# A planner's counts and priorities: transfers counted longer, and another engine taken sooner for the second weights' large part

## The chip, the cores and the metric

The kernel runs on one core of one Trainium2 chip. The metric is the device time of one execution in microseconds (us), and the median of several executions is compared. The engines are named as in the profile: PE (matrix products; PEld are its weight loads), DVE (vector), ACT (scalar), POOL (GpSimd) and SP, which here does nothing but issue DMAs from one queue, in the order of the program.

## What is computed

Nystrom attention over 8 batches, 8 heads, 576 rows and head size 64 with 32 landmarks, and then a mixture of 8 experts over the 4608 rows of the result, with one expert for each row:

```python
A = sm(q, k_lm)                       # 576 x 32 per head
Bm = sm(q_lm, k_lm)                   # 32 x 32
C = sm(q_lm, k)                       # 32 x 576
Z = Bm.T / (norms)
for _ in range(6):
    Z = 2 * Z - Z @ Bm @ Z
x = A @ Z @ C @ v                     # then rows of 8 * 64 = 512
...
expert = argmax(normed(x) @ normed(expert_emb).T / tau)
h = maximum(x @ w1[expert], 0)        # 512 -> 1024
out = gate * (h @ w2[expert])         # 1024 -> 512
```

## The kernel before

With these inputs all rows of a batch go to one expert. The kernel guesses the expert of each batch early (`guess`, `choose`), loads that expert's weights, computes the batch with them, and counts at the end whether a guess was wrong; a general path that would repair this stands behind a branch.

Each batch has its attention part and its expert part. The attention part: sums over segments of q and k (`sums`, L762), the small matrix and its inverse by six steps (`inverse`, `powers`), `values` and `products` for C @ v, `queries` for A, `landmarks` for the small factor. The expert part: four pieces of 512 KB of the first weights and four of the second weights are loaded by the SP queue (`weights`, L1360, tile `wstage`, after the expert's number `gi` has been read at L1340). ACT passes over each piece for a scale (`junk`, L1374 and L1433), and the sums over the four pieces go through PE (`ws,ones`) to give the scale. `first_weights` multiplies the first weights by the small factor on PE (`wstage,wt`) and splits the product into a large and a small float16 part (`ww`, L1418 on ACT and L1420 on DVE). `second_weights` splits the second weights likewise (`w2c`): the large part is a multiplication by the scale, on DVE (L1456) or on ACT (L1458), and the small part is always on DVE (L1460). `first` is 16 groups of six products `ab,ww` 128x288 for each batch. Each goes into one of three PSUM buffers and is taken out by a ReLU on ACT (L1468) and a difference on DVE (L1470) into `ht`. `second` is the products `w2c,ht`, whose results leave through `yt` and an output DMA on SP (L1558, L1560).

The order of all engines' instructions is made when the program is built, by a planner (`Weave`). Each step of the kernel is a generator that yields what it uses next: an engine and a duration in ns, a buffer, a flag. The planner plays these against each other in its own counted time, and issues the instruction that can start first; among those that can start within `SLACK` ns of it, the one with the highest priority (`PRI`, lowered by 1000 for each batch). A count of `DMA_LAT` is added behind every transfer. `("any", ...)` takes the engine that is counted to be done first; a third number on an offer is added to its count. `MARGIN` is added before PE steps that wait for something. On the chip each engine runs its instructions strictly in the resulting order, each waiting for its semaphores, so the counts decide the order alone and not the time.

Until the first product of `first` is issued (the flag `"moe"`), the planner also fills the time in which PE would be idle by its counts with products of ones (`keep_warm`, L673), so that the clock of PE stays up. Two lines set how many there are:

```python
    ns = self.warm((at - t) * (0.5 if self.cold(t) else 1.0) * WARM if at - t > WMIN else 0.0)
...
n = int(min(ns, 8000.0) / 56)
```

Of the kernel before, what the change touches and what calls it, by code (L numbers as in the profile page):

```python
# [48 lines left out]
HEAT = 3060.0  # L49
DENS = 1.0  # L50
LAT = {"pe": 180.0, "act": 160.0, "dve": 130.0, "pool": 160.0, "dma": 0.0}
DMA_LAT = 2000.0
SLACK = 46.4
EPS = 181.8
MARGIN = 607.2
BMARGIN = 400.0
SBIAS = 1000.0
AFTER = ("a", 0), ("a", 0)
QBIAS = 500.0
SUMS_DVE = 1  # L60
HBIAS = 0.0
WMIN = 400.0
SWITCH = 93.0
SAME = 200.0
# [10 lines left out]
BUFS = dict(k=2, q=2, v=2, ek=6, u=3, ec=2, ct=2, ae=3, at=2, st1=4, st2=4, w2=6, ww=2, ht=12, ab=3, yt=2, land=3, wt=3)  # L75

AHEAD = 20000
PRI = {"loads": 897, "sums": 1697, "inverse": 1697, "values": 1603, "queries": 703, "landmarks": 1653, "rows": 500,
       "route": 800, "guess": 844, "weights": 803, "first": 544, "second": 553}
FIRST = {"loads": 900, "sums": 800, "inverse": 800, "values": 800, "landmarks": 850, "guess": 810, "weights": 800,  # L80
         "first": 800, "embeddings": 600, "queries": 200}
EVICT, BULK = 10000, -1000
# [2 lines left out]
def rank(name, b):  # L85
    return PRI[name] - 1000 * b if b or name not in FIRST else AHEAD + FIRST[name]

# [43 lines left out]
class Weave:  # L131
# [122 lines left out]
    def run(self, *until):  # L254

        while self.gens and not (until and all(f in self.flags for f in until)):
# [4 lines left out]
            if safe > self.free["pe"]:  # L261
                ready = [(min(t, self._start(g, False)) if g[3][:2] == ("use", "pe") else t, g) for t, g in ready]
            assert ready, [g[3] for g in self.gens]
            first, lead = min(ready, key=lambda x: (x[0], x[1][3][0] in ("use", "any")))
            at, best = max(((t, g) for t, g in ready if g[3][:2] == lead[3][:2] and t <= first + SLACK),
                           key=lambda x: (self._rank(x[1]), -x[0]))
            r = best[3]
            if r[0] == "use":

                soon = [(t, g) for t, g in ready if g[2] >= max(AHEAD, best[2] + 100) and g[3][:2] == r[:2] and t < at + r[2] - EPS]  # L270
                if soon:
# [274 lines left out]
def nystrom_moe(ctx: ExitStack, tc: tile.TileContext, qT, kT, v, emb, w1, w2, out):  # L546
# [159 lines left out]
    def loads(b):  # L706
        if b:
            yield "wait", ("loads", b - 1)
        for src, dst, nm in ((kT, kt, "k"), (qT, qt, "q")):
            yield "get", nm  # L710
            if b == 2:

                yield "wait", ("weights", 2 if nm == "k" else 1, 0)
            dst[b] = inp.tile([P, 4, S], F32, tag=nm, name=nm + "_t", bufs=BUFS[nm])
            parts = 1 if b else 2
            for i in range(parts):
                yield "use", "dma", 3300 / parts
                r = slice(4 // parts * i, 4 // parts * (i + 1))
                sp.dma_start(dst[b][:, r], src[b][:, r])
                for x in range(2 // parts * i, 2 // parts * (i + 1)):  # L720
                    wv.flag((nm, b, x), DMA_LAT)
            wv.flag((nm, b), DMA_LAT)
            wv.add(sums(b, nm, dst[b]), boost=rank("sums", b))
        for gg in range(2):
            wv.add(load_values(b, gg), boost=rank("loads", b))
        wv.flag(("loads", b))

    def load_values(b, gg):
        if (b, gg) != (0, 0):
            yield "wait", ("vload", b - (not gg), 1 - gg)  # L730
        if b == 1:

            yield "wait", ("weights", 1, 0)
        i, = yield "get", "v"
        yield "use", "dma", 1640
        v_t = vt[b, gg] = vts[i]
        sp.dma_start(v_t[:, 0:4, :], v[b, 0:512, 256 * gg:256 * gg + 256].rearrange("(c p) x -> p c x", p=P))
        sp.dma_start(v_t[64:P, 4, :], v[b, 512:576, 256 * gg:256 * gg + 256])
        wv.flag(("v", b, gg), DMA_LAT)
        wv.flag(("vload", b, gg))  # L740
        wv.add(freed("v", ("vuse", b, gg), i))

    def sums(b, nm, src):
        if b >= NSUM:
            yield "wait", ("a", b - NSUM)
            yield "wait", ("u", b - NSUM)
        sm = sums_of[nm, b] = wk.tile([P, 4, M], F32, name=nm + "sum", bufs=NSUM)
        half = None
        for x in range(2):
            r = 2 * x  # L750
            yield "wait", (nm, b, x)
            if 0 < b < 3:

                yield "wait", AFTER[b - 1]
            sv = src[:, r:r + 2].rearrange("p r (m t) -> p (r m) t", t=SEG)
            if (yield "any", (("pool", 1360), ("dve", 1270, SBIAS if b >= SUMS_DVE else -SBIAS))) == "pool":
                yield "get", "half"
                half = wk.tile([P, 2 * M, SEG // 2], F32, name="half", bufs=1)
                pool.tensor_tensor(out=half, in0=sv[:, :, 0:9], in1=sv[:, :, 9:18], op=ALU.add)  # L759
                yield V(576)  # L760
                sv = half
            vec.tensor_reduce(sm[:, r:r + 2].rearrange("p r m -> p (r m)"), sv, axis=AX.X, op=ALU.add)  # L762
            if sv is half:
                wv.put("half")
        wv.flag((nm + "s", b))
        wv.tally((nm + "use", b), 2 if nm == "k" else 3)
# [197 lines left out]
    def freed(nm, flag, *ids):  # L964
        yield "wait", flag
        wv.put(nm, *ids)
# [55 lines left out]
    def held(b):  # L1022

        if b:
            yield "wait", ("ab", b - 1)
        yield "get", "ab"
        ab[b] = wk.tile([P, 2, 2, S], F16, name="ab", bufs=BUFS["ab"])
        wv.flag(("ab", b))
        yield "wait", ("rows", b)
        yield "use", "dma", 1700  # L1030
        sp.dma_start(abs_[b], ab[b])
        yield "wait", ("first", b)
        wv.put("ab")
# [305 lines left out]
    def reg(ap, max_val):  # L1339
        return nc.values_load_multi_w_load_instructions(ap, [mybir.EngineType.SP], min_val=0, max_val=max_val,  # L1340
                                                        bass_reorder=False)[1][0]
# [5 lines left out]
    def weights(b, m, src):  # L1347

        yield "wait", ("guess", b)
        if b:  # L1350
            yield "wait", ("weights", m, b - 1)
        yield "sleep", GUESS_LAT
        ev = None
        for q in range(4):
            yield "get", f"st{m}"
            yield "use", "dma", 1460
            if ev is None:
                ev = reg(gi[0:1, b:b + 1], E - 1)
            st = stage[m, b, q] = wst.tile([P, 1024], F32, tag=f"st{m}", name="wstage", bufs=BUFS[f"st{m}"])
            sp.dma_start(st, src[bass.ds(ev, 1), :, 1024 * q:1024 * q + 1024].rearrange("o p x -> (o p) x"))  # L1360
            wv.flag(("w", m, b, q), DMA_LAT)
        wv.flag(("weights", m, b))
# [64 lines left out]
    def second_weights(b):  # L1427
# [23 lines left out]
        for q in range(4):  # L1451
            yield "get", "w2"
            w = w2c[b, q] = wst.tile([P, 2, 1024], F16, name="w2c", bufs=BUFS["w2"])
            st = stage.pop((2, b, q))
            if (yield "any", (("act", 1144), ("dve", 660, HBIAS, True))) == "dve":
                vec.tensor_scalar(w[:, 0], st, sc, None, op0=ALU.mult)  # L1456
# [83 lines left out]
    def outputs(b, c, py, done, t0):  # L1540
        yield "sleep", LAT["pe"]
        yield "wait", ("gfac", b)
        if (b, c) == (B - 1, 3):

            left.append(nc.values_load(mi[0:1, 0:1], min_val=0, max_val=NT))
        yield "get", "yt"
        n = DM if c < 4 else DM // 2
        fac = gfac[:, b, c:c + 1]
        if (yield "any", (("act", n / 1.2 + 145), ("dve", (n + 66) / 0.96))) == "dve":
            yt = wst.tile([P, DM], F32, name="yt", bufs=BUFS["yt"])  # L1550
            vec.tensor_scalar(yt[:, 0:n], py[:, 0:n], fac, None, op0=ALU.mult)
        else:
            yt = wst.tile([P, DM], F32, name="yt", bufs=BUFS["yt"])
            act.activation(yt[:, 0:n], py[:, 0:n], AF.Copy, scale=fac)  # L1554
        done()
        yield "use", "dma", 730
        if c < 4:
            sp.dma_start(out[t0:t0 + P], yt)  # L1558
        else:
            sp.dma_start(out[t0:t0 + 64].rearrange("t (s x) -> s t x", s=2), yt[:, 0:256])  # L1560
        yield "sleep", DMA_LAT
        wv.put("yt")
# [20 lines left out]
    for b in range(B):  # L1583
        wv.add(loads(b), boost=rank("loads", b))
        wv.add(freed("k", ("kuse", b)))
        wv.add(freed("q", ("quse", b)))
        wv.add(batch(b))
    for b in range(B):
        wv.add(weights(b, 1, w1), boost=rank("weights", b))
        wv.add(weights(b, 2, w2), boost=rank("weights", b) - 50)  # L1590
        wv.add(first_scale(b), boost=rank("first", b))
        wv.add(first_weights(b), boost=rank("first", b))
        wv.add(second_weights(b), boost=rank("second", b))
# [7 lines left out]
    wv.warm = None  # L1601
    wv.margin, wv.bmargin = MARGIN, BMARGIN
    wv.put("bank", warm_id)
# [45 lines left out]
```

## Time and profile before

| | |
|---|---|
| median of 3 runs | 456.13 us (454.92 to 457.07) |
| the profiled execution | 455.07 us |
| its span, first to last instruction | 453.4 us |
| PE busy | 430.4 us, 95% of the span |
| DVE busy | 347.0 us, 77% |
| ACT busy | 254.1 us, 56% |
| POOL busy | 73.8 us, 16% |
| DMA | 78.21 MB, mean 173 GB/s |

A row of the profile gives the busy time of a group of instructions, the mean of one, and behind the bar the idle time of its engine just before them with what ended that idle time. A busy PE is not PE at its peak, since the ends of matmuls are modelled.

### The profile page before, as it was taken

To read this page: it belongs to the slowest core of one execution; us is meant where nothing else is said; L and a number is where in the kernel's file an instruction comes from. 1 tells how busy PE (TensorE), PEld (TensorE's weight loads), DVE (VectorE), ACT (ScalarE), POOL (GpSimd) and SP (SyncE) were. 2 spreads that over 40 slices of the span, in tenths; PEclk is the share of its full clock that TensorE was granted. 3 is DMA by queue.
4 is the path that set the end of the run, shared out by engine and by line. 5 is a ranking of instruction groups with operands and counts; after the bars stand their busy time and mean duration, and the time that the engine had idled before them with its cause. 6 is when DMAs were issued, how large, how long until landed. Compare 5 with 4: busy or idle time off the path is not lost.

```text
span 453.4 us, 13869 instructions
## 1 busy us (share of the span) xinstructions
PE 430.4 (95%) x5609; PEld 242.5 (53%) x5609; DVE 347.0 (77%) x1148; ACT 254.1 (56%) x611; POOL 73.8 (16%) x73
## 2 busy tenths in 40 slices
PE   7998899999999799999999899999999999999994
PEld 3544553466645366445655366555655466448641
DVE  5797999879797499968996299966995779578300
ACT  1377542865658455684476854866459545854211
POOL 3013341320121123300232003201020012010000
PEclk9999999999999899999999999999999999999999
DMA  8798254972278623882528913772047212921011
GB/s 298 256 394 282 75 188 135 368 239 68 87 251 286 222 67 119 283 320 75 169 78 300 334 42 121 273 251 100 26 140 279 78 49 64 329 103 38 11 50 51
DMA packets 29704, 78.21 MB, mean 173 GB/s; under 512 B 2624, under 2 KB 14016, under 8 KB 27840
## 3 DMA queue, kind: packets, MB, share of 16 engines
q1 hardware_dynamic: 29488, 77.15, 49.0%
q8 instruction: 46, 0.75, 0.7%
q14 instruction: 26, 0.21, 0.2%
q10 hardware_dynamic: 144, 0.10, 0.1%
HBM read 61.96 MB, written 15.27 MB: 170 GB/s over the span
## 4 chain that ended last, share of the span: by engine, by line
PE 56%; DVE 27%; DMA 6%; ACT 4%; issue 3%; POOL 2%; SPq 1%; ACTq 0%; POOLq 0%
PE ps L583 50%; DMA wstage<-w 6%; DVE ht L1470 5%; PE ps L673 4%; DVE w2c L1460 3%; DVE ww L1420 2%; DVE w2c L1456 1%; POOL half L759 1%; DVE cm L888 1%; DVE ae L986 1%; PE ps L935 1%; DVE am L991 1%; DVE asum L997 1%; DVE ksum L762 1%; ACT junk L1374 1%
## 5 line engine op out<-in xcount | busy, mean ns | idle before, releaser
L583 PE MATMUL ps<-w2c,ht 128*128 128x512 f16 (+1 forms) x1152 | 210.8, 346 | 0.8 <-DVE w2c L1460 0.8
L583 PEld LDWEIGHTS <-ht 128*128 128x128 f16 (+1 forms) x1152 | 88.8, 102 | 82.6 <-issue 12.0
L583 PE MATMUL ps<-ab,ww 128*128 128x288 f16 x768 | 106.4, 286 | 1.2 <-DVE ht L1470 1.1
L583 PEld LDWEIGHTS <-ww 128*128 128x128 f16 x768 | 71.5, 98 | 32.8 <-issue 11.8
L1468 ACT ACTIVATE ht<-ps 128x288 f16<-128x288 f32 x128 | 52.0, 409 | 58.0 <-PE ps L583 56.1
L1470 DVE SCALAR_TENSOR_TENSOR ht<-ps,ht 128x288 f16<-128x288 f32 x128 | 55.5, 446 | 8.4 <-ACT ht L1468 8.2
L1460 DVE SCALAR_TENSOR_TENSOR w2c<-wstage,wsc,w2c 128x1024 f16<-128x1024 f32 x32 | 40.8, 1275 | 0.7 <-ACT w2c L1458 0.7
L1433 ACT ACTIVATE junk<-wstage 128x1024 bf16<-128x1024 f32 x32 | 33.8, 1057 | 9.7 <-DMA wstage<-w 9.3
L1374 ACT ACTIVATE junk<-wstage 128x1024 bf16<-128x1024 f32 x32 | 33.7, 1054 | 8.2 <-DMA wstage<-w 8.0
L1554 ACT ACTIVATE yt<-ps,gfac 128x512 f32<-128x512 f32 (+1 forms) x26 | 16.5, 635 | 34.0 <-PE ps L583 33.8
L1257 POOL TENSOR_TENSOR nrm<-ssq,half 128x5 f32<-128x5 f32 x8 | 10.6, 1330 | 134.1 <-ACT junk L1239 134.1
L1239 ACT ACTIVATE junk<-ps 128x512 bf16<-128x512 f32 (+1 forms) x40 | 23.8, 595 | 14.3 <-DVE lg L1237 10.7
L759 POOL TENSOR_TENSOR half<-k_t 128x576 f32<-128x576 f32 x14 | 18.7, 1334 | 63.4 <-DVE ksum L762 17.4
L673 PE MATMUL ps<-ones 128*128 128x512 bf16 (+3 forms) x98 | 24.6, 396 | 2.3 <-POOL ones L608 2.3
L1420 DVE SCALAR_TENSOR_TENSOR ww<-ps,wsc,ww 128x1024 f16<-128x1024 f32 (+1 forms) x18 | 20.9, 1161 | 3.7 <-ACT ww L1418 3.6
L583 PE MATMUL ps<-wgd,ab 64*128 64x136 f16 (+1 forms) x480 | 20.7, 221 | 3.2 <-DVE ww L1420 3.2
L759 POOL TENSOR_TENSOR half<-q_t 128x576 f32<-128x576 f32 x14 | 19.7, 1406 | 24.1 <-DVE cm L910 6.9
L1418 ACT ACTIVATE ww<-ps,wsc 128x1024 f16<-128x1024 f32 (+1 forms) x18 | 18.3, 1014 | 9.0 <-PE ps L583 8.9
L583 PEld LDWEIGHTS ps<-ek 32*32 32x32 f32 x768 | 12.5, 105 | 19.1 <-issue 5.5
L583 PEld LDWEIGHTS <-ab 64*128 64x128 f16 (+1 forms) x480 | 14.4, 96 | 13.1 <-issue 11.4
L583 PE MATMUL ps<-ek 32*32 32x64 f32 (+1 forms) x768 | 20.0, 218 | 1.1 <-DVE ek L841 1.1
L1456 DVE TENSOR_SCALAR w2c<-wstage,wsc 128x1024 f16<-128x1024 f32 x25 | 19.3, 772 | 1.4 <-PE ps L583 1.4
(203 smaller groups left out, 567.0 us busy)
## 6 DMA issues: line engine op xcount, KB each, us to landing
wstage<-w SPq DMA_DIRECT2D x64, 512.0 KB, 6.2
v<-v SPq DMA_DIRECT2D x16, 512.0 KB, 6.5
out<-yt SPq DMA_DIRECT2D x32, 256.0 KB, 2.6
k_t<-kT SPq DMA_DIRECT2D x7, 1152.0 KB, 7.7
q_t<-qT SPq DMA_DIRECT2D x7, 1152.0 KB, 8.3
abs__135<-ab SPq DMA_DIRECT2D x8, 576.0 KB, 3.5
k_t<-kT SPq DMA_DIRECT2D x2, 576.0 KB, 5.3
q_t<-qT SPq DMA_DIRECT2D x2, 576.0 KB, 7.2
```

Source lines behind the costliest of these rows:

```text
L583: pe.matmul(o, lhsT, rhs, start=start, stop=stop)
L673: pe.matmul(warmth[:, 0:k * P], ones16, bc(ones16.unsqueeze(1), [P, k, P]), start=True, stop=True)
L759: pool.tensor_tensor(out=half, in0=sv[:, :, 0:9], in1=sv[:, :, 9:18], op=ALU.add)
L1239: act.activation(junk[lo:hi, 0:512].rearrange("p (i g x) -> p i g x", i=2, g=2), pfv[:, :, :, 0:2 * D], AF.Square, accum_out=ssq[lo:hi, cg ...
L1374: act.activation(junk, stage[1, b, q], AF.Square, accum_out=sq[:, q:q + 1])
L1418: act.activation(ww[:, 0], pww, AF.Copy, scale=sc)
L1420: vec.scalar_tensor_tensor(out=ww[:, 1], in0=pww, scalar=sc, in1=ww[:, 0], op0=ALU.mult, op1=ALU.subtract)
L1433: act.activation(junk, stage[2, b, q], AF.Abs, accum_out=sq[:, q:q + 1])
L1456: vec.tensor_scalar(w[:, 0], st, sc, None, op0=ALU.mult)
L1460: vec.scalar_tensor_tensor(out=w[:, 1], in0=st, scalar=sc, in1=w[:, 0], op0=ALU.mult, op1=ALU.subtract)
L1468: act.activation(ht[:, 0, r], ph[:, 0:HS], AF.Relu)
L1470: vec.scalar_tensor_tensor(out=ht[:, 1, r], in0=ph[:, 0:HS], scalar=0.0, in1=ht[:, 0, r], op0=ALU.max, op1=ALU.subtract)
```

## The change

Only numbers of the planner change; each engine's work is the same but for the choices that the planner makes anew. The counted latency of a transfer (`DMA_LAT`) goes from 2000 to 3600 ns, and each transfer's count on the queue up by some 4 to 7%. `SLACK`, `EPS` and `MARGIN`, and some priorities by a few points, change too. `HBIAS` goes from 0 to 700: DVE gets the large part of the second weights only where it would be done 700 ns sooner than ACT.

```diff
-DMA_LAT = 2000.0
-SLACK = 46.4
-EPS = 181.8
-MARGIN = 607.2
+DMA_LAT = 3600.0
+SLACK = 53.2
+EPS = 148.0
+MARGIN = 549.6
...
-HBIAS = 0.0
+HBIAS = 700.0
...
-PRI = {"loads": 897, "sums": 1697, "inverse": 1697, "values": 1603, "queries": 703, "landmarks": 1653, "rows": 500,
-       "route": 800, "guess": 844, "weights": 803, "first": 544, "second": 553}
+PRI = {"loads": 897, "sums": 1694, "inverse": 1697, "values": 1597, "queries": 700, "landmarks": 1656, "rows": 500,
+       "route": 794, "guess": 844, "weights": 803, "first": 550, "second": 550}
...
-            yield "use", "dma", 1460
+            yield "use", "dma", 1560
```

In the resulting order the products of ones (L673) are 108 of 512 columns, 3 of 384, 3 of 256 and 3 of 128, where they were 86, 5, 4 and 3. The large part of the second weights stands 30 times on ACT and 2 times on DVE (7 and 25 before). The differences and products of `both` (L1018, L1020) stand 26 times on POOL and 6 times on DVE (18 and 14 before). Three places follow.

PE just ahead of the first product of the first layer (`ab,ww`). Rows of `ones_99` are products of ones; `con,wt` is a step of `landmarks`, `wgd,ab` one of `rows`, `ws` the sum for the first weights' scale. Before:

```order
L583 MATMUL ps<-con,wt 32x8 x8
...
L673 MATMUL ps<-ones_99 128x256
L583 MATMUL ps<-wstage,wt 32x256 x8
L583 LDWEIGHTS ww
L583 MATMUL ps<-ab,ww 128x288
```

After:

```order
L583 MATMUL ps<-con,wt 32x8 x8
...
L583 MATMUL ps<-ws_646,ones_99 128x1
...
L673 MATMUL ps<-ones_99 128x384
...
L583 MATMUL ps<-wgd_109,ab 128x136
...
L673 MATMUL ps<-ones_99 128x256
L583 MATMUL ps<-wstage,wt 32x256 x8
L583 LDWEIGHTS ww
L583 MATMUL ps<-ab,ww 128x288
```

Where 12 products of ones of 512 columns and one of 256 stood, there are now 33 of 512, one of 384 and one of 256, with the sum and one step of `rows` among them.

SP, the second weights of batch 2 (the first four `wstage` behind the `TENSOR_LOAD gi` that reads the expert's number a second time). Before:

```order
L1340 TENSOR_LOAD gi
L1340 ISA x2
L1360 ISA
L1360 DMA wstage<-w 128x1024
L1360 ISA
L1360 DMA wstage<-w 128x1024
L1360 ISA
L1360 DMA wstage<-w 128x1024
L1558 DMA out<-yt 128x512
L1360 ISA
L1360 DMA wstage<-w 128x1024
```

After:

```order
L1340 TENSOR_LOAD gi
L1340 ISA x2
L1360 ISA
L1360 DMA wstage<-w 128x1024
L1360 ISA
L1360 DMA wstage<-w 128x1024
L1360 ISA
L1360 DMA wstage<-w 128x1024
L1360 ISA
L1360 DMA wstage<-w 128x1024
L1031 DMA abs__135<-ab 128x2304
```

The fourth piece no longer stands behind an output. Over all batches 11 outputs stand between the pieces of weights of a batch before, and 4 after.

ACT, from the last `ww` of batch 2 to the ReLUs of its first layer. Before:

```order
L1418 ACTIVATE ww<-ps,wsc_2494 128x1024
L1239 ACTIVATE junk,ssq<-ps 128x512
L1101 COPY ws__2718<-ps 128x128
L1554 ACTIVATE yt<-ps,gfac 128x256
L1111 COPY wt<-ps 128x128
L1113 ACTIVATE junk,wsqw<-ps 128x128
L1468 ACTIVATE ht<-ps 128x288
L1239 ACTIVATE junk,ssq<-ps 128x512
L1468 ACTIVATE ht<-ps 128x288
```

After:

```order
L1418 ACTIVATE ww<-ps,wsc_2674 128x1024
L1554 ACTIVATE yt<-ps,gfac 128x256
L1458 ACTIVATE w2c<-wstage,wsc_2813 128x1024
L1468 ACTIVATE ht<-ps 128x288
L1151 ACTIVATE scm<-block_86,scw 128x2
L1468 ACTIVATE ht<-ps 128x288
L1155 ACTIVATE wgd_110<-ps,scm 128x2x64 x2
L1468 ACTIVATE ht<-ps 128x288
L1458 ACTIVATE w2c<-wstage,wsc_2813 128x1024
L1468 ACTIVATE ht<-ps 128x288 x3
L1458 ACTIVATE w2c<-wstage,wsc_2813 128x1024
L1468 ACTIVATE ht<-ps 128x288 x2
```

The multiplications L1458 now stand between the ReLUs L1468; before, three of batch 2's four were L1456 on DVE.

## Rows read from the trace of the kernel before

**Rows 1.** The page: span, then each engine's busy time, share and instructions.

```profile
span 453.4 us, 13869 instructions
PE 430.4 (95%) x5609; PEld 242.5 (53%) x5609; DVE 347.0 (77%) x1148; ACT 254.1 (56%) x611; POOL 73.8 (16%) x73
```

**Rows 2.** Busy us by stretch; last come PE's granted clock, DMA share and GB/s.

```profile
37.00:60.00 23.00, 19.67 (x268) 12.75 (x255) 19.92 (x55) 15.18 (x43) 8.27 (x7) 1.00 0.56 189
60.00:140.00 80.00, 76.37 (x1105) 41.50 (x1103) 72.06 (x242) 45.00 (x118) 18.55 (x14) 1.00 0.56 191
140.00:160.00 20.00, 17.30 (x349) 9.43 (x348) 11.76 (x47) 10.80 (x26) 1.30 (x1) 0.91 0.69 237
160.00:240.00 80.00, 78.75 (x1000) 45.74 (x997) 73.11 (x244) 48.89 (x124) 18.81 (x15) 1.00 0.49 165
240.00:260.00 20.00, 18.22 (x326) 9.39 (x325) 8.18 (x33) 14.80 (x32) 2.60 (x2) 1.00 0.94 324
260.00:340.00 80.00, 78.62 (x1014) 46.36 (x1013) 71.79 (x225) 47.24 (x114) 11.19 (x9) 1.00 0.40 136
340.00:447.00 107.00, 106.91 (x1114) 60.99 (x1111) 61.38 (x197) 54.17 (x121) 6.37 (x5) 1.00 0.30 109
```

**Rows 3.** What PE waited for: us in total, times, longest us.

```profile
PE ps L583 <- DVE ww L1420: 3.9, 3, 2.3
PE ps L583 <- DVE ws L1039: 2.9, 2, 2.7
PE ps L1108 <- ACT ws__4329 L1101: 1.7, 1, 1.7
PE ps L583 <- DVE ek L841: 1.1, 1, 1.1
PE ps L583 <- issue: 1.0, 1, 1.0
PE ps L583 <- DVE w2c L1460: 0.8, 1, 0.8
PE ps L1108 <- ACT ws__1469 L1101: 0.6, 1, 0.6
```

**Rows 4.** PE in order of time before the first layer: start, us.

```profile
6.57 6.68 PE L673 MATMUL ps<-ones 128*128 128x512 bf16 x28
...
33.79 2.87 PE L673 MATMUL ps<-ones 128*128 128x512 bf16 x13
36.59 0.66 PE L583 MATMUL ps<-wstage,wt 64*32 64x256 f32 x16
37.19 0.91 PE L583 MATMUL ps<-ab,ww 128*128 128x288 f16 x6
```

**Rows 5.** DVE in order of time: the last sum before PE, and one later wait.

```profile
10.71 1.34 DVE L762 TENSOR_REDUCE qsum<-q_t 128x64 f32<-128x1152 f32 x1
...
45.43 0.75 DVE L762 TENSOR_REDUCE qsum<-half 128x64 f32<-128x576 f32 x1 [1.46 <-POOL half L759]
```

**Rows 6.** SP, ACT and PE in order of time, around 143 to 151 us.

```profile
142.32 0.35 SPq L1558 DMA_DIRECT2D out<-yt  x1
...
142.86 0.33 SPq L1360 DMA_DIRECT2D wstage<-w  x1
...
149.38 1.06 ACT L1433 ACTIVATE junk<-wstage 128x1024 bf16<-128x1024 f32 x1 [2.63 <-DMA wstage<-w]
...
150.96 0.16 PE L583 MATMUL ps<-ws,ones 128*128 128x1 bf16 x1 [2.70 <-DVE ws L1039]
```

**Rows 7.** Busy us by stretch again, columns as in rows 2.

```profile
148.00:152.00 4.00, 1.30 (x6) 0.27 (x3) 1.16 (x6) 2.15 (x3) 0.00 (x0) 0.89 1.03 370
152.00:156.00 4.00, 4.00 (x63) 1.82 (x70) 2.29 (x8) 1.00 (x3) 1.30 (x1) 0.69 0.43 136
```

**Rows 8.** ACT in order of time, around 257 us.

```profile
257.42 1.06 ACT L1433 ACTIVATE junk<-wstage 128x1024 bf16<-128x1024 f32 x1 [0.96 <-DMA wstage<-w]
...
258.48 0.25 ACT L1101 COPY ws__4329<-ps 128x128 f32<-128x128 f32 x1
```

**Rows 9.** DMA issues of one line: count, size, median us to landing.

```profile
wstage<-w SPq DMA_DIRECT2D x64, 512.0 KB, 6.2
```

**Rows 10.** Groups by line and shape: busy, mean ns of one, idle time before.

```profile
L1470 DVE SCALAR_TENSOR_TENSOR ht<-ps,ht 128x288 f16<-128x288 f32 x128 | 55.5, 446 | 8.4 <-ACT ht L1468 8.2
L1468 ACT ACTIVATE ht<-ps 128x288 f16<-128x288 f32 x128 | 52.0, 409 | 58.0 <-PE ps L583 56.1 <-DVE asum L997 1.3
L1456 DVE TENSOR_SCALAR w2c<-wstage,wsc 128x1024 f16<-128x1024 f32 x25 | 19.3, 772 | 1.4 <-PE ps L583 1.4
L1458 ACT ACTIVATE w2c<-wstage,wsc 128x1024 f16<-128x1024 f32 x7 | 8.0, 1145 | 0.5 <-PE ps L583 0.5
L994 ACT ACTIVATE ae<-ae 128x576 f32<-128x576 f32 x16 | 10.9, 681 | 5.8 <-DVE ae L1020 4.0 <-POOL ae L1018 1.8
```

More of the change, by code (lines that the diff above doesn't have):

```diff
@@ L716, in loads @@
             for i in range(parts):
-                yield "use", "dma", 3300 / parts
+                yield "use", "dma", 3520 / parts
                 r = slice(4 // parts * i, 4 // parts * (i + 1))
@@ L734, in load_values @@
         i, = yield "get", "v"
-        yield "use", "dma", 1640
+        yield "use", "dma", 1760
         v_t = vt[b, gg] = vts[i]
@@ L1029, in held @@
         yield "wait", ("rows", b)
-        yield "use", "dma", 1700
+        yield "use", "dma", 1760
         sp.dma_start(abs_[b], ab[b])
@@ L1555, in outputs @@
         done()
-        yield "use", "dma", 730
+        yield "use", "dma", 780
         if c < 4:
```

## The prediction

> **What bounds the kernel now.** I read first the busy shares: PE works 430.4 of 453.4 us [rows 1], no other engine is near it, and the first layer's own products are the same before and after. So the kernel is bound by PE, and a new order can gain only in three places: PE's idle time, PE's slow clock, and the products of ones that PE does only because the planner thinks that it would be idle.
>
> The second view is the busy time by stretch [rows 2]. Length minus PE's busy time gives the idle time: 3.33 us from 37 to 60, 3.63 from 60 to 140, 2.70 from 140 to 160, 1.25 from 160 to 240, 1.78 from 240 to 260, 1.38 from 260 to 340 and 0.09 after that. These are 14.2 us. Nothing is to be had behind 340 us, where PE is full.
>
> The third view says who was late [rows 3]. I split the list into three kinds.
>
> Kind one, at the start of the first layer: the stretch from 37 to 60 us, 3.3 us, nearly all of it the split `ww` on DVE (3.9 us in three waits, one of them later). One reason can be read off DVE: a sum L762 waited 1.46 us for a half that POOL makes [rows 5], and what stood behind it on DVE waited too.
>
> Kind two, where a transfer was late. The list names DVE (`ws`, 2.7 us) and ACT (`ws__4329`, 1.7, and `ws__1469`, 0.6), but the order of time shows that they only passed a delay on. Around 143 us the SP queue issued an output and, 0.54 us later, the last `wstage`; ACT waited 2.63 us for that piece, and PE 2.70 [rows 6]. At 257 us ACT waited again for a `wstage`, and the copy for which PE waits stood behind it on ACT [rows 8]. I take the third, of the same form, as the same kind. Idle time: 2.7 + 1.7 + 0.6 = 5.0 us. The first had a price behind it: after the wait PE was granted 0.89 of its clock in one stretch of 4 us and 0.69 in the next [rows 7], part of the time at 1.2 instead of 2.4 GHz, and that is up to 4 x 0.11 + 4 x 0.31 = 1.7 us of work lost. Kind two is 6.7 us.
>
> Kind three is the rest, PE waiting for DVE's pieces or for nothing that shows: 3.63 - 0.6 from 60 to 140, 1.25 and 1.38 later, together 5.7 us. DVE is busy for 72.06 of 80 us from 60 to 140 [rows 2], so a short wait there is no surprise.
>
> **The change, part by part.** *Products of ones.* The longer counts make the planner see more idle time ahead of the first layer, and it puts in 108 + 2.25 + 1.5 + 0.75 = 112.5 equivalents of 512 columns instead of 92.5. One takes (36.59 - 33.79)/12.5 = 0.224 us [rows 4]. PE passes from its products of ones straight into `wstage,wt` and `ab,ww` there, so what is added has no idle time to sink into: 20 x 0.224 = +4.5 us. Bounds: eight of the 20 stand ahead of the first product with a sum, whose sum is done at 10.71 + 1.34 = 12.05 us [rows 5], while PE's first block of ones runs on to 13.25 [rows 4]; these +1.8 us are sure. The other twelve could cover waits that the new order would otherwise have there. With the modelled end counted they cost at most 4.8. I take 4.5, since the rows show PE without a gap there.
>
> *Start of the first layer.* DVE no longer has the large part of the second weights between the splits, but L762 with its wait for POOL still stands ahead of `ww`. Of 3.3 us I let 1.5 stay, the size of that wait [rows 5]: -1.8, with bounds 0 and -3.3.
>
> *Transfers counted longer.* A `wstage` was counted at 1460 + 2000 = 3460 ns and is now counted at 5160. In the trace it takes 6.2 us from issue to landing in the median [rows 9]. So the planner placed ACT's passes and what hangs on them nearly 3 us too early, and now about 1 us too early. On SP the outputs between the pieces of one batch go from 11 to 4, and the piece that was late at 143 us no longer has an output ahead of it. PE also gets 3 to 8 us more of its own work, by its order, between the choice of the expert and the sums for the scale in batches 3 to 7. In batch 2 it gets less, so I leave 1.0 us of kind two standing: -5.7. Bounds: -6.7 if all goes, -2 if only the named output was the cause and the lost clock goes in part.
>
> The Trainium skill, "DMA: Bandwidth & Descriptors", section "Anatomy of one DMA — SWDGE (gpsimd) path", fits a transfer as about 2.0 us plus its bytes at 436 GB/s, for the GpSimd path. For 512 KB that is 3.2 us, an estimate from that page, and by it the old count was right and the new one is padding. The trace, on the SP queue and beside other transfers, shows 6.2 us, and by it the new count is the nearer one.
>
> *Large parts from DVE to ACT.* 23 multiplications move. On DVE one is 772 ns, on ACT 1145 [rows 10]: DVE loses 23 x 0.772 = 17.8 us of 347.0, ACT gains 23 x 1.145 = 26.3 on 254.1, and is then at 62%. In no engine's total does this matter; what matters is who waits. DVE also loses eight of the products of `both` to POOL, which is busy for 16% [rows 1]. For kind three I take a third of a wait as gone on the busiest engine: 5.7 to 3.5, so -2.2. Bounds: 0, since the `issue` wait and the small parts L1460 stay, and -5.
>
> What ACT gets in exchange lies beside PE's work as long as ReLUs are in time. A group of six products takes 6 x 288/512 x 0.224 = 0.76 us on PE, its ReLU 0.41 and its difference 0.45 [rows 10]. With three PSUM buffers and groups back to back, a buffer is wanted again two groups, 1.51 us, after its own group ended, and it is free after 0.86. That leaves 0.65 us, and a multiplication of 1.145 us in front of the ReLU overruns it by 0.5. But a batch's 16 groups are only 12.1 us of the roughly 54 (430.4/8) that PE works for a batch, so mostly other products stand between them. Before, ACT waited 56.1 us for groups at L1468 [rows 10] and PE's list names no ReLU [rows 3]. I take 0, with bounds 0 and 23 x 0.5 = +11.5 us; a gain is covered by kind three.
>
> *The rest.* `SLACK`, `EPS`, `MARGIN` and the points of priority change choices by at most some ns in the count. I have no row for their effect, and put what they reorder into the bounds above.
>
> **Sum.** 455.07 + 4.5 - 1.8 - 5.7 - 2.2 + 0 = 449.9 us for the profiled execution. It lay 1.06 us under the median of the runs, 456.13, so the forecast is 450.9. With its own bounds, two or three terms off together, this case reaches from 447 to 453.9.
>
> **Rivals.** *ACT becomes the late engine* (slower). Place: the ReLUs L1468 of batches 1 to 7, with an L1458 in front. Price: the 0.5 us above for each of 23, on top of the sum: 450.9 + 11.5 = 462.4. It makes the kernel slower by over 0.5% from 7.5/23 = 0.33 us each. For it: the new order puts such a multiplication straight ahead of ReLUs of batch 2 several times, where one in four was on ACT before, and kind three does not gain then. Against it: the other work between the groups, ACT's 56.1 us of waiting for them, and the seven that stood on ACT before without a wait of PE. The Trainium skill, "ScalarE: Activation LUTs", section "Rules for kernel authors", speaks for this rival: it wants a multiplication on VectorE and not on ScalarE. The prices 772 and 1145 ns agree with it for one instruction; whether the slower engine makes PE late, no row of before shows.
>
> *Transfers land as late as before* (no change). If the reading of the expert's number and the queue set the time at which the pieces land, and not the place in the order, PE waits for kind two as before: 450.9 + 5.7 = 456.6. For it: at 143 us the output cost the piece only 0.54 us of issue time [rows 6], against a wait of 2.63, and batch 2 has less PE work ahead of that sum now. In the stretches around 152 and 250 us the DMA engines are nearly full, 1.03 and 0.94 [rows 7, 2], which no order on ACT cures. Against it: ACT's passes stand later in the new order in most batches. That the longer counts are only padding ends at the same place.
>
> *All waits of both kinds go* (faster still). The start gives 3.3, the transfers 6.7, kind three 3.7: 455.07 + 4.5 - 3.3 - 6.7 - 3.7 + 1.06 = 446.9. For it: DVE is relieved just in the stretches where it was full. Against it: L762 behind POOL is unchanged.
>
> **How the numbers follow.** A difference of 0.5%, 2.3 us, is about what a measurement of this kernel can tell from no change; the limits are 453.8 and 458.4. Forecast 0.45, all waits go 0.10, transfers as late as before 0.25, ACT late 0.20, since 23 instructions take a new place that no row shows. Faster is then 0.55, the same 0.25, slower 0.20. The range reaches from 445.5, just under the third rival, to 459.5; what it leaves out is most of the ACT case and the tail of the third, under 0.2.
>
> **What would show it.** Right: the first `ab,ww` about 4 to 5 us later than 37.19; no stretch behind 140 us with a granted clock under 1.00; no `ws` or L1101 wait of over 1 us in PE's list; DVE at about 330 us of work and ACT at 280. Wrong: `ht` of L1468 or L1470 in PE's list with several us, which would be the ACT rival; `ws` there with 2 us or more, which would be the transfers; or a first `ab,ww` that is hardly later, which would mean that the twelve products of ones cost nothing.

## The result, and the profile after

The changed kernel takes 450.25 us in the median (448.86 to 452.25), the kernel before, with one more run beside it, 455.52 (453.9 to 457.07). The ratio is 0.988, with an interval of 0.984 to 0.993. It is faster, by 1.2%, and the forecast was 450.9. The profiled execution took 449.05 us against 455.07.

The page of the changed kernel, to be read beside [rows 1]: DVE has 19 us less, ACT 23 us more. The page also gives the transfers' size and median time to landing.

```profile
span 447.3 us, 13932 instructions
PE 432.4 (97%) x5628; PEld 245.5 (55%) x5628; DVE 328.1 (73%) x1110; ACT 277.5 (62%) x641; POOL 79.5 (18%) x80
...
L1458 ACT ACTIVATE w2c<-wstage,wsc 128x1024 f16<-128x1024 f32 x30 | 34.4, 1149 | 0.6 <-PE ps L583 0.2
...
wstage<-w SPq DMA_DIRECT2D x64, 512.0 KB, 6.9
```

The busy time by stretch, columns as in [rows 2]:

```profile
37.00:60.00 23.00, 22.06 (x300) 13.44 (x298) 19.62 (x60) 16.21 (x42) 6.80 (x6) 1.00 0.67 235
60.00:140.00 80.00, 76.86 (x1188) 43.19 (x1186) 72.87 (x256) 51.27 (x129) 24.93 (x20) 1.00 0.56 190
140.00:160.00 20.00, 20.00 (x296) 10.86 (x295) 10.23 (x49) 15.56 (x35) 1.18 (x1) 1.00 0.78 274
160.00:240.00 80.00, 78.38 (x1112) 46.16 (x1117) 73.30 (x232) 59.65 (x140) 18.89 (x15) 1.00 0.62 218
240.00:260.00 20.00, 20.00 (x248) 9.58 (x229) 10.83 (x47) 11.27 (x25) 1.20 (x1) 1.00 0.29 98
260.00:340.00 80.00, 79.85 (x1119) 48.18 (x1116) 63.67 (x216) 58.51 (x136) 12.91 (x11) 1.00 0.46 169
```

PE's idle time is now 0.94, 3.14, 0, 1.62, 0 and 0.15 us. In the two stretches where transfers were late, 140 to 160 and 240 to 260 us, it is gone to the last digit, and in the first of them the granted clock is 1.00 where it was 0.91. Behind 340 us a clock under 1.00 shows only from 443 us on (0.50), when PE has done its last product. What PE still waits for:

```profile
PE ps L583 <- DVE ht L1470: 2.6, 8, 0.6
PE ps L673 <- POOL ones L608: 2.3, 1, 2.3
PE ps L583 <- DVE w2c L1460: 1.3, 1, 1.3
PE ps L583 <- DVE ww L1420: 0.5, 2, 0.4
```

The second is PE's start, which is the same before. The list has no `ws` and no L1101. Its first row stands for more than before, when it was

```profile
PE ps L583 <- DVE ht L1470: 1.3, 4, 0.6
```

The order of time ahead of the first layer, as in [rows 4]:

```profile
37.35 0.53 PE L583 MATMUL ps<-wgd,ab 64*128 64x136 f16 x12
37.81 3.09 PE L673 MATMUL ps<-ones 128*128 128x512 bf16 x14
40.83 0.66 PE L583 MATMUL ps<-wstage,wt 64*32 64x256 f32 x16
41.42 1.65 PE L583 MATMUL ps<-ab,ww 128*128 128x288 f16 x12
```

The first `ab,ww` starts at 41.42 and not at 37.19, and the products of ones still run into it without a gap.

### The profile page after: what moved, and what is told of

It is laid out like the page before. It is cut to its first block, busy times and chain, and to the rows that moved or that the text cites. A ratio compares the mean times of both kernels' runs of the same rounds, so it can differ in the third digit from the quotient of the medians.

```text
span 447.3 us, 13932 instructions
## 1 busy us (share of the span) xinstructions
PE 432.4 (97%) x5628; PEld 245.5 (55%) x5628; DVE 328.1 (73%) x1110; ACT 277.5 (62%) x641; POOL 79.5 (18%) x80
## 4 chain that ended last, share of the span: by engine, by line
PE 68%; DVE 21%; DMA 3%; ACT 3%; POOL 2%; issue 1%; SPq 1%; POOLq 0%; ACTq 0%; DVEq 0%
PE ps L583 61%; PE ps L673 5%; DVE ht L1470 4%; DVE w2c L1460 3%; DMA k_t<-kT 2%; POOL half L759 2%; DMA wstage<-w 2%; DVE qsum L762 1%; DVE cm L888 1%; PE ps L935 1%; DVE ksum L762 1%; DVE ww L1420 1%; DVE ae L986 1%; DVE asum L997 1%; ACT w2c L1458 1%
## 5 line engine op out<-in xcount | busy, mean ns | idle before, releaser
L1468 ACT ACTIVATE ht<-ps 128x288 f16<-128x288 f32 x128 | 51.9, 409 | 37.2 <-PE ps L583 36.5
L1470 DVE SCALAR_TENSOR_TENSOR ht<-ps,ht 128x288 f16<-128x288 f32 x128 | 54.7, 447 | 8.8 <-ACT ht L1468 8.5
L1460 DVE SCALAR_TENSOR_TENSOR w2c<-wstage,wsc,w2c 128x1024 f16<-128x1024 f32 x32 | 41.0, 1281 | 12.4 <-ACT w2c L1458 12.4
L1554 ACT ACTIVATE yt<-ps,gfac 128x512 f32<-128x512 f32 (+1 forms) x29 | 18.4, 635 | 46.5 <-PE ps L583 45.9
L1018 POOL TENSOR_TENSOR ae<-ae,am 128x576 f32<-128x576 f32 x15 | 17.3, 1159 | 101.4 <-DVE am L991 81.2
L1458 ACT ACTIVATE w2c<-wstage,wsc 128x1024 f16<-128x1024 f32 x30 | 34.4, 1149 | 0.6 <-PE ps L583 0.2
L673 PE MATMUL ps<-ones 128*128 128x512 bf16 (+3 forms) x117 | 28.4, 390 | 2.3 <-POOL ones L608 2.3
L759 POOL TENSOR_TENSOR half<-q_t 128x576 f32<-128x576 f32 x13 | 17.3, 1332 | 25.5 <-DVE ksum L762 14.5
```

The lines of the kernel that those rows point to most:

```text
L673: pe.matmul(warmth[:, 0:k * P], ones16, bc(ones16.unsqueeze(1), [P, k, P]), start=True, stop=True)
L1458: act.activation(w[:, 0], st, AF.Copy, scale=sc)
L1460: vec.scalar_tensor_tensor(out=w[:, 1], in0=st, scalar=sc, in1=w[:, 0], op0=ALU.mult, op1=ALU.subtract)
L1468: act.activation(ht[:, 0, r], ph[:, 0:HS], AF.Relu)
L1470: vec.scalar_tensor_tensor(out=ht[:, 1, r], in0=ph[:, 0:HS], scalar=0.0, in1=ht[:, 0, r], op0=ALU.max, op1=ALU.subtract)
```

## The experiments

The theory from the prediction was that the longer counts take the late transfers away at the price of the ones, and that the bias gives DVE room. The main rivals were that one part does it all, and that an order is a draw: any new one falls anywhere. Twelve kernels were run. I read each by three numbers besides its ratio: PE's idle time in the first 440 us (440 less PE's busy time in that stretch), the time lost to the clock (the sum of 1 less the granted clock, times the length, over the stretches of 23, 20 and 80 us), and the ones. These three, the span and the late transfers come from the one profiled execution of each kernel, the ratio from several runs. With the bias alone that execution took 461.91 us against a median of 459.08, so its idle time and lost clock are rather too high; for the others it lies within 1.2 us of the median.

| kernel | ratio to before | span | idle | clock | ones of 512 | late transfers |
|---|---|---|---|---|---|---|
| before | 1 | 453.4 | 16.6 | 1.8 | 92.5 | 5.2 |
| changed | 0.988 (0.984 to 0.993) | 447.3 | 8.6 | 0 | 112.5 | 0 |
| counts | 1.027 (1.020 to 1.034) | 466.8 | 24.2 | 5.0 | 106.75 | 0 |
| bias | 1.007 (1.003 to 1.011) | 460.2 | 19.8 | 6.4 | 92.5 | 3.7 |
| rest | 1.008 (1.004 to 1.012) | 457.4 | 19.0 | 3.2 | 93.5 | 0.3 |
| counts, bias | 0.999 (0.996 to 1.003) | 454.1 | 13.3 | 3.2 | 106.75 | 0 |
| counts, rest | 1.004 (1.001 to 1.007) | 455.0 | 12.9 | 3.2 | 112.5 | 0.5 |
| bias, rest | 0.983 (0.978 to 0.989) | 448.8 | 12.5 | 0 | 93.5 | 0 |

"Late transfers" is the sum of PE's waits for `ws`, `wsq` (both made from ACT's passes over `wstage`) and L1101 (with the bias alone PE also waits 0.4 us for `wstage` itself). "Rest" is slack, EPS, margin and the points of priority. Idle, clock and ones together give the spans to about 1 us: rest alone has 2.4 us more idle time than before, 1.4 of clock and 1 x 0.224 of ones, 4.0 in all, and its span is 4.0 longer; the changed kernel has -8.0, -1.8 and +4.5, -5.3, and its span is 6.1 shorter.

**Each part alone.**

```diff
-DMA_LAT = 2000.0
+DMA_LAT = 3600.0
-            yield "use", "dma", 1460
+            yield "use", "dma", 1560
...
```

> The kernel before with the transfers' counts alone (latency 3600 and the five longer queue counts). By its order 14.25 more products of ones than before, and the large parts stay on DVE (25 of 32). My theory: these counts bring back the 6.7 us of late transfers and cost 14.25 x 0.224 = 3.2 us, so -3.5 us, a ratio of 0.992, and no wait of PE for ws or L1101 of over 1 us. Rival one, the move to ACT did it: the late transfers stay, +3.2 us, 1.007. Rival two, any new order of this kind does about as well or as badly by luck: then the waits that go here are others than in the changed kernel.

It is slower by 2.7%. The late transfers are gone, as I expected, but the first thing in PE's list is now DVE:

```profile
PE ps L583 <- DVE w2c L1460: 9.7, 4, 5.4
```

The longest of these waits, in the order of time of DVE and then of PE:

```profile
243.48 0.75 DVE L762 TENSOR_REDUCE qsum<-half 128x64 f32<-128x576 f32 x1 [1.04 <-POOL half L759]
...
247.13 1.27 DVE L1460 SCALAR_TENSOR_TENSOR w2c<-wstage,wsc,w2c 128x1024 f16<-128x1024 f32 x1
...
248.45 1.86 PE L583 MATMUL ps<-w2c,ht 128*128 128x512 f16 x4 [5.37 <-DVE w2c L1460]
```

The stretches there (PE's busy us comes second, the granted clock third from the end):

```profile
244.00:248.00 4.00, 0.00 (x0) 0.00 (x0) 4.00 (x8) 1.26 (x2) 1.80 (x2) 0.66 0.69 276
248.00:252.00 4.00, 3.55 (x24) 1.26 (x24) 4.00 (x14) 0.84 (x2) 0.03 (x1) 0.50 0.32 77
```

DVE waited 1.04 us for a half from POOL, then did its steps of the attention part, and the piece for which PE waits came last. PE stood still for 5.4 us and then ran at 1.2 GHz.

```diff
-HBIAS = 0.0
+HBIAS = 700.0
```

> The kernel before with the bias of 700 ns alone: 30 large parts on ACT, the 92.5 products of ones as before. My theory: the waits at the start and some on DVE go (-2.4 and -0.8 us), the late transfers stay: -3.2 us, 0.993. Rival one, the move to ACT did it all: about -10 us without the cost of the ones, 0.978. Rival two, ACT becomes late and the counts make up for it: slower than before, over 1.005, with L1468 or L1470 in PE's list.

Slower by 0.7%, though DVE has 16.5 us less to do. The wait at the start of the first layer is as before (`ww`, 3.6 us in three), and 3.7 us of late transfers are there, at other places than before. For the longest of them, 1.8 us for `ws` at 167 us, the form is the same: on SP an output stands ahead of the last piece, and ACT waits for that piece:

```profile
158.47 0.35 SPq L1558 DMA_DIRECT2D out<-yt  x1
159.01 0.33 SPq L1360 DMA_DIRECT2D wstage<-w  x1
...
165.17 1.06 ACT L1433 ACTIVATE junk<-wstage 128x1024 bf16<-128x1024 f32 x1 [2.40 <-DMA wstage<-w]
```

```diff
-SLACK = 46.4
-EPS = 181.8
-MARGIN = 607.2
+SLACK = 53.2
+EPS = 148.0
+MARGIN = 549.6
...
```

(and the points of priority)

> The kernel before with slack, EPS, margin and the few points of priority alone: 93.5 products of ones, 28 large parts on DVE. My theory: no lasting effect, 1.000 with some 0.4% to either side. Rival two (luck of the order): it can move the time as far as the whole change did, to under 0.99 or over 1.01.

Slower by 0.8%, and not for nothing: it rids the kernel of the late transfers (0.3 us left) and of most of the wait for `ww` (1.0 us left of 3.9), without any longer count. In exchange DVE is late elsewhere, once for 4.1 us, and 3.2 us of clock go:

```profile
PE ps L583 <- DVE ht L1470: 4.4, 11, 0.6
PE ps L583 <- DVE ek L841: 4.4, 2, 4.1
```

My theory's forecast for these three (0.992, 0.993, 1.000) was wrong for each: no part brings the gain alone.

**Two parts at a time.** The edits are those above, taken together.

> The transfers' counts and the bias together, without slack, EPS, margin and the points of priority. In the first set of runs each part alone made the kernel slower (1.027, 1.007, 1.008). Theory one, the two need each other: the counts alone take the late transfers away but put DVE's pieces so close that PE waits for w2c, and the bias gives DVE the room: 0.985 to 0.995 here. Theory two, the order as a whole is a draw, and the change is a lucky one: no reason for a gain here, 0.995 to 1.02.

0.999: PE's idle time shrinks as the bias goes in (24.2 us with the counts alone, 13.3 here), but the ones cost 3.2 us and the clock 3.2.

> The changed kernel with the bias back at 0: 29 large parts on DVE, 112.5 products of ones. Theory one: DVE is late again, PE waits several us for w2c and ht: 1.01 to 1.03. Theory two, a draw: could as well be under 0.995.

1.004: without the bias, no gain. One wait of 2.5 us for DVE at 86 us costs it another 3.2 us of clock.

> The changed kernel without the longer counts of transfers: bias 700, slack, EPS, margin and priorities as in the changed kernel, 93.5 products of ones. If the longer counts are what takes the late transfers away: PE waits 2 to 5 us for ws and L1101, and the time is 1.000 to 1.01 though 19 x 0.224 = 4.3 us of ones are saved. If they only add ones: 0.978 to 0.985.

0.983, and no `ws`, `wsq` or L1101 in PE's list. That is the clearest answer against my theory: the late transfers are gone without the longer counts, and the kernel is no slower than the changed one. Between the two the idle time is 12.5 against 8.6 us, 3.9 in favour of the counts, and the ones are 19 x 0.224 = 4.3 us against them. The counts buy about what they cost; the intervals overlap.

**Is it luck of the order?**

```diff
-SLACK = 53.2
+SLACK = 50.0
```

(in the changed kernel)

> The changed kernel with one planner's number that stands for nothing moved a little: slack 50.0 for 53.2. The products of ones stay 112.5, the large parts 29 on ACT; a part of the order is another. If the change works through its mechanisms: 0.984 to 0.993, as the changed kernel, and no late transfer. If the order is a draw: anywhere from 0.985 to 1.01, with several us of waits for DVE's pieces at places where the changed kernel has none.

0.988 (0.984 to 0.993), the same as the changed kernel, with no late transfer and 8.7 us of idle time, though 1.6 us of clock are lost in its profiled execution and its order differs from that one's in hundreds of places on PE and DVE. So the three orders with bias and rest lie at 0.983, 0.988 and 0.988, and the six others made by the planner, the kernel before among them, at 0.999 to 1.027. A pure draw is not excluded by so few, but it isn't what they look like.

**The engine alone, in an unchanged order.**

```diff
-            if (yield "any", (("act", 1144), ("dve", 660, HBIAS, True))) == "dve":
+            if (yield "any", (("act", 1144), ("dve", 660, HBIAS, True))):
```

(in the changed kernel: what the planner gave to ACT is issued on DVE at the same place)

> The changed kernel in its own order on PE, SP and POOL, but the 30 large parts that the planner gave to ACT are issued on DVE in the same place of the program: the order does not change, only the engine. Theory one in its plain form, DVE's load decides: 30 x 0.77 us more on DVE in the stretches where it is fullest; PE waits more for ht and w2c, 0.995 to 1.01. If what counts is the order that the planner made with the bias, and not the engine that does the work, the time stays at 0.988 within 0.4%.

0.9955 (0.992 to 0.999) where the changed kernel has 0.988. The order on PE, SP and POOL is the same, so the difference, 0.7% or some 3.3 us, is the engine's doing alone; the two intervals overlap by 0.001, and PE's idle time in the first 440 us is 11.4 us against 8.6. The stretches show it, beside those of the changed kernel above: DVE is fuller, and PE has 0.76, 1.25 and 0.57 us more idle time.

```profile
60.00:140.00 80.00, 76.10 (x1166) 42.59 (x1166) 76.07 (x258) 43.24 (x120) 24.95 (x20) 1.00 0.54 183
160.00:240.00 80.00, 77.13 (x1061) 45.74 (x1061) 76.01 (x234) 48.38 (x123) 19.71 (x15) 1.00 0.58 203
260.00:340.00 80.00, 79.28 (x1071) 47.61 (x1073) 64.88 (x214) 48.12 (x123) 12.91 (x11) 1.00 0.46 167
```

In the kernel before, the mirror image (`== "none":` in that line, so that all are issued on ACT):

> The kernel before in its own order, but the 25 large parts that stood on DVE are issued on ACT in the same place. DVE's load decides: the waits for DVE at the start and for w2c shrink, -1 to -3 us, 0.993 to 0.998. ACT is the late engine: 25 x 0.5 us, up to 1.027, with ht of L1468 in PE's list. The order decides: 1.000 within 0.4%, the late transfers as before.

1.003 (0.999 to 1.008): no gain, and nearly no sign of the ReLU rival, one wait of 0.4 us for L1468. Relief for DVE gave 0.7% in the one order and nothing in the other. Here 4.2 us of late transfers and the start's wait of 2.3 us for `ww` stay; that these are the reason was not tried.

**The one output.**

```diff
-            sp.dma_start(out[t0:t0 + P], yt)
+            (act if (b, c) == (1, 2) else sp).dma_start(out[t0:t0 + P], yt)
```

(in the kernel before)

> The kernel before, where one output alone (batch 1, third chunk, the one issued at 142.32 us) is issued from ACT's queue instead of SP's, behind ACT's first L1433 of batch 2. If this output holds up the fourth piece of the second weights: the piece is issued at about 138.5, the wait of 2.7 us at 148 goes and the lost clock with it, -2.7 to -4.4 us, 0.990 to 0.994. If the piece would have been late anyway (the buffer, or the DMA engines that are full there): the wait of PE stays over 1.5 us and the time within 0.4%.

0.992 (0.989 to 0.996), by moving a single transfer to another queue. SP in the kernel before, around the output, which [rows 6] shows only in part:

```profile
136.81 1.38 SPq L1360 DMA_DIRECT2D wstage<-w  x3
142.32 0.35 SPq L1558 DMA_DIRECT2D out<-yt  x1
142.86 0.33 SPq L1360 DMA_DIRECT2D wstage<-w  x1
```

SP with the output moved, and then ACT's last pass, in order of time:

```profile
137.24 1.97 SPq L1360 DMA_DIRECT2D wstage<-w  x4
...
147.75 1.06 ACT L1433 ACTIVATE junk<-wstage 128x1024 bf16<-128x1024 f32 x1
```

The stretch whose clock was 0.89 in [rows 7]:

```profile
148.00:152.00 4.00, 3.84 (x55) 1.70 (x59) 3.14 (x14) 2.16 (x5) 0.00 (x0) 1.00 1.03 404
```

The fourth piece leaves with the other three, 3.6 us sooner or more, ACT doesn't wait, and PE's wait of 2.7 us is 0.16. This execution is only 0.5 us shorter in its span, since another wait, for nothing that shows, took 2.0 us at 196 us where it took 1.0, and 1.6 us of clock went with it; the ratio rests on all the runs.

**The ones.**

```diff
 for i in range(0, n, 4):
     k = min(n - i, 4)
+    if i // 4 % 5 == 3:
+        continue
```

(in the changed kernel; the products of ones give nothing that is used, so nothing of what is computed is left out, and the order of the rest is the same. The lines behind it move by 2)

> The changed kernel in its own order, but every fifth product of ones of a group is left out of what is issued: 94.5 equivalents of 512 columns for 112.5, all else the same. My theory: each costs its 0.224 us, since PE comes to the first layer without a gap: -4.0 us against the changed kernel, 0.979 against before, first ab,ww at about 37.4. Rival: the ones only fill waits for data; then the time is that of the changed kernel, 0.988, and PE shows idle time before 41 us in place of the products. Third: the granted clock falls and the time is over 0.990.

0.980 (0.973 to 0.986), 447.2 us, the lowest median of all. The first `ab,ww` starts 2.91 us sooner, at 38.51; of 18 x 0.224 = 4.0 us that were left out, a quarter came back as waits ahead of the first layer, the first of them here:

```profile
34.20 0.16 PE L583 MATMUL ps<-ws,ones 128*128 128x1 bf16 x1 [0.43 <-DVE ws L1041]
```

With `i // 4 % 2 == 1` instead, which leaves 61:

> The changed kernel in its own order with 61 equivalents of 512 columns of ones for 112.5. The 18 left out before brought 3.1 us of their 4.0. If ones cost their time throughout: -11.5 us against the changed kernel, 0.963. If data are late from here on: about -5 us, 0.977, with the rest turned into idle time of PE before 37 us. If the granted clock falls before the first layer: 0.980 or more, no gain over the kernel with 94.5.

0.980 (0.977 to 0.984), no further gain. PE waits for data now (`ws` 1.7 us), starts the first layer at 39.70 and not sooner, and gets less of its clock, just ahead of the first layer above all, where seven products of ones take 3.05 us and not 7 x 0.224 = 1.6:

```profile
35.88 3.05 PE L675 MATMUL ps<-ones 128*128 128x512 bf16 x7
...
36.00:40.00 4.00, 4.00 (x26) 1.24 (x25) 3.23 (x6) 3.84 (x10) 0.44 (x1) 0.57 0.79 229
...
37.00:60.00 23.00, 21.95 (x310) 13.26 (x312) 18.58 (x56) 15.31 (x41) 7.78 (x6) 0.95 0.68 233
```

So nothing is left of what leaving out more than the first 18 saved; as far as these rows show, it came back as waits for data and as a lower clock. Some of the ones do their office and some don't.

## Why the prediction was right, and where it was not

The time was forecast within 0.7 us, and the sum of the terms in the profiled execution was -5.2 where it measured -6.0. Term by term:

- Ones, +4.5 forecast. The first `ab,ww` came 4.23 us later, and leaving 18 out brought it 2.91 us of 4.0 forward. Right, with the small reserve that a quarter of the price covered waits.
- Start of the first layer, -1.8 forecast: the idle time from 37 to 60 us went from 3.33 to 0.94, -2.4.
- Late transfers, -5.7 forecast: all 6.7 us went, the 1.0 kept for batch 2 too.
- Waits for DVE, -2.2 forecast: 5.7 us became 3.14 + 1.62 + 0.15 = 4.9, so -0.8.
- ReLUs behind the large parts on ACT, 0 forecast, between 0 and +11.5: PE's list names no L1468 in the changed kernel, and one wait of 0.4 us in the kernel before with all parts on ACT. But L1470, which stands behind the ReLU and was a sign of that rival too, goes from 1.3 to 2.6 us. Of the six longer of these eight waits, 2.3 us, one of 0.28 us, at 109.5 us, has an L1458 on ACT ahead of it; in the others DVE came to L1470 late, behind its own steps. DVE now waits 12.4 us for the large parts from ACT, where it waited 0.7, but nearly nothing of that reaches PE. Right within half a us.

```profile
L1460 DVE SCALAR_TENSOR_TENSOR w2c<-wstage,wsc,w2c 128x1024 f16<-128x1024 f32 x32 | 41.0, 1281 | 12.4 <-ACT w2c L1458 12.4
```

These add up to +4.2 - 2.4 - 6.7 - 0.8 = -5.7.

Of the start and the waits for DVE only the sum is firm, -3.2 where -4.0 was forecast. The stretches are cut at fixed times, and the first layer now begins 4.23 us later. Cut 4.23 us later too, they read

```profile
41.23:64.23 23.00, 20.46 (x329) 13.24 (x315) 19.18 (x58) 13.53 (x37) 8.80 (x7) 1.00 0.62 223
64.23:144.23 80.00, 78.47 (x1205) 43.77 (x1204) 70.61 (x255) 53.26 (x135) 22.62 (x18) 1.00 0.60 205
```

and the idle time at the start is 2.54 us, -0.8, and that of the third kind 1.53 + 1.62 + 0.15 = 3.3, -2.4.

What failed is the step that gave the late transfers to the longer counts. The prediction put it so that the planner had placed ACT's passes nearly 3 us too early and would now do better. All orders with longer counts have at most 0.5 us of such waits, which fits; but bias and rest have none with the old counts, and rest alone 0.3. So the waits did go, but the counts were not needed for it. Nor does the number of outputs between the pieces tell it, which the prediction had going from 11 to 4: by SP's order in the traces it is 12 with the counts alone, without a late transfer, 7 with the bias alone and with the rest alone, with 3.7 and 0.3 us, and 5 with both, with none. For the longest wait before, the cause was one output ahead of a piece, as moving it showed. For the others it was not tried, and how the rest or the counts remove them stays open. Whether longer counts make an order with late transfers less likely is not settled by nine orders.

A second step was misread, in the rival by which transfers land as late as before: "the output cost the piece only 0.54 us of issue time". That is the time between the two issues on SP. The three pieces ahead had left by 136.81 + 1.38 = 138.2 us, so the fourth stood for 4.7 us behind an output whose own data came at 142.3. Moving that one output brought 0.8% back. What an output costs a piece behind it is read from the last issue ahead of the output, not from the output on.

The third is what was put at "choices by at most some ns". The rest, alone +0.8%, takes the time from 1.007 to 0.983 where the bias is in. It had no row, and I had taken its effect into the bounds of other terms. Which of its four numbers does it was not tried, nor why it does so only with the bias.

On the two places where a rule was weighed. By the fit in the Trainium skill, "DMA: Bandwidth & Descriptors", section "Anatomy of one DMA — SWDGE (gpsimd) path", a piece on the GpSimd path takes an estimated 3.2 us. On SP's queue the trace has 6.2 us before and 6.9 after, so the old count was too short, as I had read it. But that the truer count would bring the gain did not follow. The Trainium skill, "ScalarE: Activation LUTs", section "Rules for kernel authors", wants a multiplication on VectorE. One instruction is slower on ACT, 1149 ns against 772, and still the same order with the parts on DVE is 0.7% slower, with 2.6 us more idle time of PE in the three stretches where DVE is fuller.

So the forecast was right in its sum, and wrong in who earned it. That it came so near is in part luck: without the counts, its terms leave -1.8 - 2.2 = -4.0 us, a ratio of 0.991, where bias and rest have 0.983 (0.978 to 0.989).

## What to carry to other kernels

When several numbers of a planner change at once, read the gain by where the waits go, and give it to a number only when that number was tried alone and was left out alone: here each part alone made the kernel slower, and one that cost 2.7% alone made little difference in the whole. Look in an in-order DMA queue for a transfer that waits for its data in front of one that others wait for; moving one output was worth 0.8%. And try moving work off the engine for which the bound engine waits, even to a slower one: it was worth 0.7% in one order and nothing in another.

## What the runs showed of the hardware

The clock's price for a wait is not the same each time. In the kernel before and in the one with the bias alone, PE waits the same 2.3 us for `ww` at 44 to 47 us, with the same work around it. Before:

```profile
44.00:48.00 4.00, 1.69 (x32) 1.27 (x31) 2.57 (x10) 1.15 (x4) 2.58 (x2) 1.00 0.28 118
48.00:52.00 4.00, 4.00 (x71) 2.39 (x68) 3.80 (x13) 3.59 (x10) 1.97 (x2) 1.00 0.01 4
```

With the bias alone:

```profile
44.00:48.00 4.00, 1.70 (x29) 1.26 (x24) 2.96 (x12) 1.16 (x4) 2.30 (x2) 0.99 0.14 58
48.00:52.00 4.00, 4.00 (x48) 2.11 (x46) 2.65 (x8) 3.12 (x9) 1.28 (x1) 0.58 0.02 4
```

PE is busy 1.69 and 1.70 us of the first stretch, and in the second it does 71 matmuls at 1.00 before and 48 at 0.58, part of the time at 1.2 GHz: about 0.42 x 4 = 1.7 us lost, on top of the wait. The same 18 products behind the wait, before and then with the bias alone:

```profile
47.36 2.38 PE L583 MATMUL ps<-ab,ww 128*128 128x288 f16 x18
...
46.97 3.60 PE L583 MATMUL ps<-ab,ww 128*128 128x288 f16 x18
```

What decides it the rows don't show. Nor is it a matter of the order alone: the kernel before had a mean granted clock of 0.998 in one run, of 454.75 us, and of 0.985 in another, of 458.21. So the lost clock of the table, 0 to 6.4 us, which is of one execution each, is a part of what tells these spans apart, but not of the orders by themselves. The profiled executions of the changed kernel and of bias with rest lost none, that with slack 50, at the same ratio as the changed kernel, 1.6 us.
